# Block-sparse attention and a gated MLP on one core: how the first head pair is loaded and masked, and how the in-projection is dealt out

## The chip, the core and the metric

The kernel runs on one core of a Trainium2 chip. The core has a matrix engine (TensorE, PE in the profile; its weight loads are PEld), a vector engine (DVE), a scalar engine for activations (ACT), a general engine (POOL) and an engine that here only issues transfers (SP). Each engine works through its own list of instructions in order and waits on semaphores for the others. Transfers are issued from the list of SP or of ACT and are carried out by 16 DMA engines. [...]

The metric is the device time of one execution in microseconds (us). The kernel before took 222.43 us, the median of 13 runs (221.78 to 223.98).

## The reference

Attention over 4 batches, 8 heads, 768 positions and 64 dimensions, with a mask in blocks of 32, and then a gated MLP whose spatial matrix mixes the positions:

```python
scores = scale * np.matmul(q, k.transpose(0, 1, 3, 2))
mask = np.abs(blk_i - blk_j) <= 1
mask = mask | (blk_i == 0) | (blk_j == 0) | (blk_i == n_blocks - 1) | (blk_j == n_blocks - 1)
for qb in range(n_blocks):
    for kb in sampled_blocks[qb]:            # 3 for each of 24 blocks
        mask[qb*block:(qb+1)*block, kb*block:(kb+1)*block] = True
attn = softmax(np.where(mask, scores, -1e9))
x = np.matmul(attn, v)                       # heads side by side: (4, 768, 512)

h = np.maximum(x @ w_in, 0.0)                # 512 -> 1024
u, v = h[..., :512], h[..., 512:]
v_n = (v - mean(v)) / np.sqrt(var(v) + 1e-6)
v_s = np.einsum('ts,bsd->btd', w_spatial, v_n) + b_spatial[None, :, None]
out = (u * v_s) @ w_out
```

## The kernel before, in words

**Attention.** q and k of a head pair are loaded as fp32 with positions on partitions (st_q, st_k, 128x768 for two heads), cast to bf16 (nat_q, nat_k) and transposed to 64 dimensions by 768 positions (qt, kt). The first batch is transposed on PE (tr_head for pair 0, one head at a time; tr_pair in three thirds for pairs 1 to 3), later pairs by DMA (tr_dma and split_pair). The mask is part of the matmul: below the 64 dimensions, qt and kt have 24 more rows. In kt they hold ind, which says which key block a position is in; in qt they hold bm times ind, where the 24x24 matrix bm is 0 for an allowed pair of blocks and -300 for any other. All heads need the same rows. Before the change ind is built on POOL (memset, affine_select) and rearranged by DVE; bm is worked out by DVE from iotas and the sampled blocks (allowed, samp_f); two matmuls make qt's rows in PSUM (mq), ACT copies them into head 0, and mask_rows (DVE, heads 1 to 5 in part) and mask_dma (SP queue, heads 4 to 7 of kt and 6 and 7 of qt) repeat them for the other heads.

**Order of the attention.** The first batch (N0 = 48 steps g) works by halves of the queries: qk_exp_half(g) makes two score matmuls 88x128 by 88x384 and one exponential of 128x768 on ACT; steps 0 to 2 belong to head 0, 3 to 5 to head 1, and so on to step 23; steps 24 to 47 repeat this for the second half of the queries. av_half runs 6 steps behind (LAG0), and xtr_half transposes the normalised result of a pair (xn) to xt. Later batches use qk_exp with whole heads, six steps for each head, and av 7 steps behind (LAG).

**The MLP.** moe_units(b) lists the matmuls of a batch's MLP as units, 108 for each batch: twelve in-projections of 4 units (v0 to v5 and u0 to u5, one for each 128 positions), six spatial products of 6, six out-projections of 4. The string order gives the sequence of the in-projections. They take turns at two PSUM banks (tags moe0 and moe1), which the transposes use too. v_post copies a v product to vsb with a ReLU and takes its mean and variance (DVE: vsb, stats, mv); after v2 and v5, POOL makes rstd for three of them, and normalize (DVE, vn) is queued in norm_q with the number of products that must be done before it. normalize_next is called in the middle of every product and after every u. u_post copies a u product to un, on ACT except for u0 of batch 0.

**How units are dealt out.** In the first batch one unit goes to each step from g = 29 on. At the change of batch none is dealt in steps 48 to 54; from g = 55 (N0 + 7) the 89 that are left are spread over 50 steps. Batches 1 and 2 spread 108 over 48 and 52 steps; the last batch's MLP runs after the attention, back to back, over six banks.

**The start.** The first tiles of pair 0 are loaded by heads: head 0 of k and q on ACT's queue, samp_i and head 1 on SP's. keep_warm issues matmuls on a tile of zeros, whose result nobody reads: 8 of 512 columns first, 6 of 128 after the q transposes, and 2 of 128 in each of the first six steps.

These lines set the order at the two places that the change touches:

```python
keep_warm(8, 512)                                       # L199
...
tr_head(0, "k", dve_copy)                               # L281
act_copy(kt[0][D:KR, :], ind)
...                                                     # mq, two matmuls, act_copy into qt[0]
tr_head(0, "q", dve_copy)
keep_warm(6, 128)
...
norm_q.extend((i, products[0] + 2) for i in range(tcc - 2, tcc + 1))   # L496
...
if g == N0 + 7:
    slots_left = 50                                     # L682
```

Of the kernel before, what the change touches and what calls it, by code (L numbers as in the profile page):

```python
# [10 lines left out]
FP32 = mybir.dt.float32  # L11
BF16 = mybir.dt.bfloat16
I32 = mybir.dt.int32
# [13 lines left out]
def kernel(  # L27
# [146 lines left out]
    nc.scalar.dma_start(out=stk[:, 0:1], in_=dram(k, 0, 0, 1))  # L174
    nc.scalar.dma_start(out=stq[:, 0:1], in_=dram(q, 0, 0, 1))
    nc.sync.dma_start(out=samp_i, in_=_listify(sampled_blocks).bitcast(I32))
    nc.sync.dma_start(out=stk[:, 1:2], in_=dram(k, 0, 1, 1))
    nc.sync.dma_start(out=stq[:, 1:2], in_=dram(q, 0, 1, 1))
# [6 lines left out]
    allowed = const.tile([NB, NB], FP32)  # L185
    tiny = const.tile([128, 1], FP32)
    nc.vector.memset(warm, 0.0)
    nc.gpsimd.memset(ind_nat, 0.0)
# [5 lines left out]
    def keep_warm(n, cols):  # L194
        for _ in range(n):
# [3 lines left out]
    keep_warm(8, 512)  # L199
# [4 lines left out]
    nc.gpsimd.affine_select(out=ind_nat, in_=ind_nat, compare_op=ALU.not_equal, fill=1.0,  # L204
                            base=0, pattern=[[-1, NB], [0, BLK]], channel_multiplier=1)
# [6 lines left out]
    colidx = const.tile([NB, NB], FP32)  # L212
    nc.gpsimd.iota(colidx, pattern=[[1, NB]], base=0, channel_multiplier=0,
                   allow_small_or_imprecise_dtypes=True)
    make_identity(nc, ident)
    for s in range(NG):
        nc.gpsimd.memset(vv[s][:, :, :, D:VA], 1.0)
    nc.gpsimd.memset(mhalf, -0.5)

    nat_tile(0, "q"), nat_tile(0, "k")  # L220
    nc.vector.tensor_copy(out=ind, in_=ind_nat.rearrange("b (p c) -> b c p", c=NCH))
# [3 lines left out]
    nc.vector.tensor_scalar(out=edge, in0=edge, scalar1=0.0, scalar2=None, op0=ALU.is_equal)  # L225
    nc.vector.tensor_tensor(out=diff, in0=diff, in1=diff, op=ALU.mult)
    nc.vector.tensor_scalar(out=allowed, in0=diff, scalar1=1.0, scalar2=edge,
                            op0=ALU.is_le, op1=ALU.max)
    nc.vector.memset(allowed[:, 0:1], 1.0)
    nc.vector.memset(allowed[:, NB - 1:NB], 1.0)  # L230
    samp_f = const.tile([NB, 2 * NR], FP32)
    nc.vector.tensor_copy(out=samp_f, in_=samp_i)
    for r in range(NR):
        nc.vector.scalar_tensor_tensor(out=allowed, in0=colidx,
                                       scalar=samp_f[:, 2 * r:2 * r + 1], in1=allowed,
                                       op0=ALU.is_equal, op1=ALU.max)
    bm = const.tile([NB, NB], BF16)
    nc.vector.tensor_scalar(out=bm, in0=allowed, scalar1=1.0, scalar2=-MASK_NEG,
                            op0=ALU.subtract, op1=ALU.mult)
    cast_qk(0, "q", slice(0, 1), nc.vector)  # L240
    cast_qk(0, "k", slice(0, 1), nc.scalar)
# [39 lines left out]
    tr_head(0, "k", dve_copy)  # L281
    act_copy(kt[0][D:KR, :], ind)
    mq = psum.tile([128, 1024], FP32, tag="sc", bufs=2, name="mq")
    for hf in range(2):
        nc.tensor.matmul(out=mq[0:NB, hf * 512:hf * 512 + HALF], lhsT=bm,
                         rhs=ind[:, hf * HALF:(hf + 1) * HALF], start=True, stop=True)
    act_copy(qt[0][D:KR, :].rearrange("p (b c) -> p b c", b=2),
             mq[0:NB].rearrange("p (b c) -> p b c", b=2)[:, :, 0:HALF])
# [150 lines left out]
    def moe_units(b):  # L439
# [19 lines left out]
        def normalize_next():  # L459
            if norm_q and norm_q[0][1] <= products[0]:  # L460
                normalize(norm_q.popleft()[0])

        def add(n, operands, post):
# [4 lines left out]
            def step(i):  # L468
# [5 lines left out]
                if i == n // 2:  # L474
                    normalize_next()
# [5 lines left out]
        def v_post(tcc, ps):  # L481
# [8 lines left out]
            if tcc % 3 == 2:  # L490
# [5 lines left out]
                norm_q.extend((i, products[0] + 2) for i in range(tcc - 2, tcc + 1))  # L496
# [7 lines left out]
        def u_post(tcc, ps):  # L504
            if b == 0 and tcc == 0:
# [4 lines left out]
            normalize_next()  # L510

        def in_proj(tcc, cols, post):
# [5 lines left out]
                 "v0 v1 u0 v2 u1 v3 u2 v4 v5 u3 u4 u5")  # L518
# [53 lines left out]
    def mask_rows(nm, h0, h1):  # L572
        t = kt_all if nm == "k" else qt_all
        nc.vector.tensor_copy(out=t[D:KR, h0:h1, :],
# [160 lines left out]
```

## Time and profile before

| | |
|---|---|
| median of 13 runs | 222.43 us (221.78 to 223.98) |
| the profiled execution | 223.36 us, span 221.6 us |
| PE busy | 213.0 us of the span |
| ACT busy | 177.0 us |
| DVE busy | 135.9 us |
| POOL busy | 66.9 us |
| first exponential begins | 8.72 us |
| first score matmul of step 48 begins | 45.60 us |

The span runs from the first to the last instruction; the time of the execution also holds what lies around it. A view with a start and a duration is a timeline: start, duration, engine, line, operation, output and inputs, count, and in brackets how long the engine was idle before it and which instruction released it. The profile models the ends of matmuls, so successive matmuls overlap in the figures. Line numbers of helpers stand for all their callers: L472 is every MLP matmul, L313 and L348 are score matmuls of later batches and of the first, L262 a head's transposes, L196 a warmer, L124 a cast, L574 and L579 are the copies and transfers of mask rows.

### The profile page before, as it was taken

How to read it: one execution, taken by the hardware profiler on the slowest of the kernel's cores; microseconds unless marked ns; L12 is line 12 of the kernel's file. 1: busy time of each engine (PE TensorE's matmuls, PEld its weight loads, DVE VectorE, ACT ScalarE, POOL GpSimd, SP SyncE). 2: the span in 40 equal slices, each digit the busy share in tenths (PEclk: the TensorE clock that was granted, in tenths of full speed). 3: DMA queues.
4: the chain of work that ended last, by engine and by line, in shares of the span. 5: the costliest groups of instructions: out<-in, count | busy, mean ns of one | idle time of the engine just before them, and what ended most of it. 6: DMA issues, size and time to landing. Idle time of an engine off the chain costs nothing.

```text
span 221.6 us, 5292 instructions
## 1 busy us (share of the span) xinstructions
PE 213.0 (96%) x2122; PEld 127.7 (58%) x2122; DVE 135.9 (61%) x302; ACT 177.0 (80%) x245; POOL 66.9 (30%) x89
## 2 busy tenths in 40 slices
PE   7989999999999999999899999999899999999993
PEld 2567666665666666666465656565565565544551
DVE  5488527856886635377798635376896433675532
ACT  5489999999999889988979878888989885266351
POOL 6457879523187040400609001200602000022000
PEclk9999999999999999999999999999999999999999
DMA  6999999999995498979772369998321124620016
GB/s 179 336 300 394 397 264 340 171 117 315 237 366 113 113 275 181 276 249 268 219 186 108 72 131 230 219 280 211 62 48 26 37 50 84 221 91 0 0 54 230
DMA packets 59460, 41.26 MB, mean 186 GB/s; under 512 B 42524, under 2 KB 54956, under 8 KB 59436
## 3 DMA queue, kind: packets, MB, share of 16 engines
q1 hardware_dynamic: 59148, 40.54, 69.8%
q10 hardware_dynamic: 288, 0.39, 0.6%
q8 instruction: 16, 0.26, 0.5%
q14 instruction: 8, 0.07, 0.1%
HBM read 24.38 MB, written 6.29 MB: 138 GB/s over the span
## 4 chain that ended last, share of the span: by engine, by line
PE 84%; DVE 8%; ACT 5%; issue 1%; POOL 1%; ACTq 0%; POOLq 0%
PE ps_moe L472 32%; PE ps L313 18%; PE ps_av L329 11%; PE ps L348 7%; ACT a_all L317 4%; PE ps_t L472 4%; PE ps_sc L472 4%; PE ps_av L364 3%; PE wps L196 2%; DVE kt_all L278 2%; DVE kt_all L302 1%; PE ps_moe L262 1%; DVE vsb L485 1%; DVE vn L499 1%; DVE qt_all L278 1%
## 5 line engine op out<-in xcount | busy, mean ns | idle before, releaser
L317 ACT ACTIVATE a_all<-ps 128x768 bf16<-128x768 f32 x144 | 114.6, 815 | 16.1 <-PE ps L313 7.4
L313 PE MATMUL ps<-qt_all,kt_all 88*128 88x384 bf16 x288 | 70.3, 325 | 0.8 <-ACT a_all L317 0.7
L329 PEld LDWEIGHTS <-a_all 128*128 128x128 bf16 x864 | 46.1, 97 | 35.6 <-issue 2.2
L329 PE MATMUL ps_av<-vv,a_all 128*128 128x65 bf16 x864 | 50.8, 194 | 0.0
L472 PE MATMUL ps_moe<-w_in_t,xt 128*128 128x512 bf16 x160 | 48.8, 379 | 1.4 <-DVE vsb L485 1.3
L352 ACT ACTIVATE a_all<-ps 128x768 bf16<-128x768 f32 x48 | 35.5, 813 | 3.5 <-PE ps L348 3.2
L472 PE MATMUL ps_moe<-vn,w_spt 128*128 128x512 bf16 x120 | 35.4, 378 | 0.0
L472 PEld LDWEIGHTS <-xt 128*128 128x128 bf16 x192 | 18.6, 97 | 16.3 <-DVE xt L386 0.5
L492 POOL TENSOR_SCALAR std<-mv 128x3 f32<-128x3 f32 x8 | 1.9, 241 | 82.3 <-DVE mv L489 73.3
L535 DVE SCALAR_TENSOR_TENSOR gn<-ps_moe,b_col,un 128x512 bf16<-128x512 f32 x20 | 15.0, 749 | 17.1 <-PE ps_moe L472 16.9
L348 PE MATMUL ps<-qt_all,kt_all 88*128 88x384 bf16 x96 | 23.8, 330 | 1.2 <-DVE qt_all L278 0.7
L124 POOL CAST nat_k<-st_k 128x768 bf16<-128x768 f32 (+1 forms) x14 | 11.5, 819 | 41.2 <-DMA st_k<-in_k_dram 32.4
L472 PE MATMUL ps_moe<-w_out_t,gt 128*128 128x512 bf16 x80 | 23.1, 378 | 0.1
L313 PEld LDWEIGHTS <-kt_all 88*128 88x128 bf16 x288 | 19.3, 98 | 1.6 <-issue 1.0
L472 PEld LDWEIGHTS <-w_spt 128*128 128x128 bf16 x144 | 13.7, 97 | 10.6
L364 PEld LDWEIGHTS <-a_all 128*128 128x128 bf16 x288 | 15.1, 98 | 6.2
L488 DVE BATCH_NORM_STATS2 stats<-vsb 128x6 f32<-128x512 bf16 x24 | 16.6, 693 | 1.5 <-ACT vsb L483 0.8
L364 PE MATMUL ps_av<-vv,a_all 128*128 128x65 bf16 x288 | 17.0, 194 | 0.0
L499 DVE TENSOR_SCALAR vn<-vsb,mv,rstd 128x512 bf16<-128x512 bf16 x24 | 12.8, 560 | 5.0 <-POOL rstd L494 4.8
L485 DVE TENSOR_SCALAR vsb<-ps_moe 128x512 bf16<-128x512 f32 x18 | 12.3, 686 | 5.3 <-PE ps_moe L472 4.7
L555 DVE COPY osb<-ps_moe 128x512 f32<-128x512 f32 x10 | 6.9, 692 | 11.5 <-PE ps_moe L472 11.4
L395 DVE TENSOR_TENSOR xn<-ps_av,rc 128x384 bf16<-128x384 f32 x24 | 13.4, 557 | 0.8
(98 smaller groups left out, 219.7 us busy)
## 6 DMA issues: line engine op xcount, KB each, us to landing
out_dram<-osb SPq DMA_DIRECT2D x24, 256.0 KB, 2.7
st_v<-in_v_dram SPq DMA_DIRECT2D x14, 384.0 KB, 5.8
st_k<-in_k_dram SPq DMA_DIRECT2D x13, 384.0 KB, 4.7
st_q<-in_q_dram SPq DMA_DIRECT2D x13, 384.0 KB, 3.9
wst<-in_moe_w_spatial_dram SPq DMA_DIRECT2D x3, 768.0 KB, 9.6
wst<-in_moe_w_in_dram SPq DMA_DIRECT2D x4, 512.0 KB, 8.6
wst<-in_moe_w_out_dram SPq DMA_DIRECT2D x2, 512.0 KB, 7.5
wst<-in_k_dram SPq DMA_DIRECT2D x2, 384.0 KB, 9.2
```

The costliest lines, as they stand in the source:

```text
L313: nc.tensor.matmul(out=ps[:, hf * 512:hf * 512 + HALF], lhsT=kt[j % H][:, ci * 128:(ci + 1) * 128], rhs=qt[j % H][:, hf * HALF:(hf + 1) * ...
L317: nc.scalar.activation(out=a_ref[j][:, ci, :].rearrange("p (b c) -> p b c", b=2), in_=ps.rearrange("p (b c) -> p b c", b=2)[:, :, 0:HALF], ...
L329: nc.tensor.matmul(out=av_ref[j][:, qc, :], lhsT=a_ref[j][:, ci, qc * 128:(qc + 1) * 128], rhs=vv[p % NG][:, h, ci, :], start=(ci == 0), s ...
L348: nc.tensor.matmul(out=ps[:, u * 512:u * 512 + HALF], lhsT=kt[j][:, ci * 128:(ci + 1) * 128], rhs=qt[j][:, grp * HALF:(grp + 1) * HALF], s ...
L352: nc.scalar.activation(out=a_ref["half", gh][:, 2 * i:2 * i + 2, :], in_=ps.rearrange("p (b c) -> p b c", b=2)[:, :, 0:HALF], func=AF.Exp, ...
L364: nc.tensor.matmul(out=av_ref["half", gh][:, qc, :], lhsT=a_ref["half", gh][:, ci, qc * 128:(qc + 1) * 128], rhs=vv[p][:, h, ci, :], start ...
L395: nc.vector.tensor_tensor(out=xn_ref[p][:, :, h, :], in0=ps[:, :, 0:D], in1=rc.to_broadcast([128, NCH, D]), op=ALU.mult)
L472: nc.tensor.matmul(out=box[0], lhsT=lhs, rhs=rhs, start=(i == 0), stop=(i == n - 1))
L485: nc.vector.tensor_scalar(out=vsb[:, tcc, :], in0=ps, scalar1=0.0, scalar2=None, op0=ALU.max)
L488: nc.vector.bn_stats(out=stats, in_=vsb[:, tcc, :])
L499: nc.vector.tensor_scalar(out=vn[:, tcc, :], in0=vsb[:, tcc, :], scalar1=mv[:, tcc, 0:1], scalar2=rstd[:, tcc:tcc + 1], op0=ALU.subtract, ...
L535: nc.vector.scalar_tensor_tensor(out=gn[:, tcc, :], in0=ps, scalar=b_col[:, tcc:tcc + 1], in1=un[:, tcc, :], op0=ALU.add, op1=ALU.mult)
```

## The change

- Pair 0 is loaded whole: k on ACT's queue, q on SP's behind samp_i.
- ind_nat's memset moves from POOL to DVE; POOL's iotas come before its affine_select; ACT rearranges ind in place of DVE.
- bm is made from a static part that does not depend on the samples, and one comparison of all three samples, a maximum and one more operation.
- The two mask products are issued apart, the first before head 0's transposes; k of head 0 is cast on DVE and its transposed form copied by ACT.
- kt's mask rows of heads 1 to 3 are copied by POOL, those of 4 to 7 by one transfer straight from ind. qt's rows are copied by DVE by halves of the queries, at the start and in steps 6, 20 and 23.
- Warmers: 6 of 512 for 8, 3 of 128 added after the first mask product, none in steps 0 to 2. Both of head 1's transposes come in step 0, pair 1's in steps 1 and 2.
- In-projection units are dealt in steps 48 to 55 too, none in step 56, and the 81 left over 48 steps from step 57.
- norm_q counts half products: the first three normalisations become due one product later, the last three half a product earlier. u1 and u2 of batch 0 go to DVE. Batches 1 and 2 alternate v and u to the end.

```diff
-    nc.scalar.dma_start(out=stk[:, 0:1], in_=dram(k, 0, 0, 1))
-    nc.scalar.dma_start(out=stq[:, 0:1], in_=dram(q, 0, 0, 1))
+    nc.scalar.dma_start(out=stk, in_=dram(k, 0, 0, 2))
     nc.sync.dma_start(out=samp_i, in_=_listify(sampled_blocks).bitcast(I32))
-    nc.sync.dma_start(out=stk[:, 1:2], in_=dram(k, 0, 1, 1))
-    nc.sync.dma_start(out=stq[:, 1:2], in_=dram(q, 0, 1, 1))
+    nc.sync.dma_start(out=stq, in_=dram(q, 0, 0, 2))
...
-    nc.gpsimd.memset(ind_nat, 0.0)
+    nc.vector.memset(ind_nat, 0.0)
...
-    keep_warm(8, 512)
+    keep_warm(6, 512)
...
-    nat_tile(0, "q"), nat_tile(0, "k")
-    nc.vector.tensor_copy(out=ind, in_=ind_nat.rearrange("b (p c) -> b c p", c=NCH))
...
-    nc.vector.tensor_scalar(out=allowed, in0=diff, scalar1=1.0, scalar2=edge,
+    nc.vector.tensor_scalar(out=static, in0=diff, scalar1=1.0, scalar2=edge,
                             op0=ALU.is_le, op1=ALU.max)
-    samp_f = const.tile([NB, 2 * NR], FP32)
-    nc.vector.tensor_copy(out=samp_f, in_=samp_i)
-    for r in range(NR):
-        nc.vector.scalar_tensor_tensor(out=allowed, in0=colidx,
-                                       scalar=samp_f[:, 2 * r:2 * r + 1], in1=allowed,
-                                       op0=ALU.is_equal, op1=ALU.max)
+    nc.vector.tensor_scalar(out=static, in0=static, scalar1=1.0, scalar2=-MASK_NEG,
+                            op0=ALU.subtract, op1=ALU.mult)
+    for c in (0, NB - 1):
+        nc.vector.memset(static[:, c:c + 1], 0.0)
+    nat_tile(0, "q"), nat_tile(0, "k")
+    nc.scalar.activation(out=ind, in_=ind_nat.rearrange("b (p c) -> b c p", c=NCH),
+                         func=AF.Copy)
+    hit = const.tile([NB, NR, NB], FP32)
+    nc.vector.tensor_tensor(
+        out=hit, in0=colidx.to_broadcast([NB, NR, NB]),
+        in1=samp_i.rearrange("b (r t) -> b r t", t=2)[:, :, 0:1].to_broadcast([NB, NR, NB]),
+        op=ALU.is_equal)
+    hits = const.tile([NB, NB], FP32)
+    nc.vector.tensor_reduce(out=hits, in_=hit.rearrange("b r n -> b n r"), op=ALU.max,
+                            axis=mybir.AxisListType.X)
     bm = const.tile([NB, NB], BF16)
-    nc.vector.tensor_scalar(out=bm, in0=allowed, scalar1=1.0, scalar2=-MASK_NEG,
-                            op0=ALU.subtract, op1=ALU.mult)
-    cast_qk(0, "q", slice(0, 1), nc.vector)
-    cast_qk(0, "k", slice(0, 1), nc.scalar)
+    nc.vector.scalar_tensor_tensor(out=bm, in0=hits, scalar=0.0, in1=static,
+                                   op0=ALU.is_equal, op1=ALU.mult)
+    nc.scalar.activation(out=kt[0][D:KR, :], in_=ind, func=AF.Copy)
+    cast_qk(0, "k", slice(0, 1), nc.vector)
+
+    def kt_mask(h):
+        nc.gpsimd.tensor_copy(out=kt[h][D:KR, :], in_=ind)
+
+    def qt_mask(h0, h1, grp):
+        cols = slice(grp * HALF, (grp + 1) * HALF)
+        nc.vector.tensor_copy(out=qt_all[D:KR, h0:h1, cols],
+                              in_=qt_all[D:KR, 0:1, cols].to_broadcast([NB, h1 - h0, HALF]))
...
+    cast_qk(0, "k", slice(1, 2), nc.gpsimd)
...
-    tr_head(0, "k", dve_copy)
-    act_copy(kt[0][D:KR, :], ind)
     mq = psum.tile([128, 1024], FP32, tag="sc", bufs=2, name="mq")
-    for hf in range(2):
+
+    def mask_product(hf):
         nc.tensor.matmul(out=mq[0:NB, hf * 512:hf * 512 + HALF], lhsT=bm,
                          rhs=ind[:, hf * HALF:(hf + 1) * HALF], start=True, stop=True)
-    act_copy(qt[0][D:KR, :].rearrange("p (b c) -> p b c", b=2),
-             mq[0:NB].rearrange("p (b c) -> p b c", b=2)[:, :, 0:HALF])
+        act_copy(qt[0][D:KR, hf * HALF:(hf + 1) * HALF],
+                 mq[0:NB, hf * 512:hf * 512 + HALF])
+
+    mask_product(0)
+    keep_warm(3, 128)
+    cast_qk(0, "q", slice(0, 1), nc.vector)
+    tr_head(0, "k", act_copy)
+    mask_product(1)
     tr_head(0, "q", dve_copy)
     keep_warm(6, 128)
...
-        def normalize_next():
-            if norm_q and norm_q[0][1] <= products[0]:
+        def normalize_next(time):
+            if norm_q and norm_q[0][1] <= time:
                 normalize(norm_q.popleft()[0])
...
-                    normalize_next()
+                    normalize_next(2 * products[0])
...
-                norm_q.extend((i, products[0] + 2) for i in range(tcc - 2, tcc + 1))
+                norm_q.extend((i, 2 * products[0] + (6 if tcc == 2 else 3)) for i in range(tcc - 2, tcc + 1))
...
-            if b == 0 and tcc == 0:
+            if b == 0 and tcc < NCH // 2:
...
-            normalize_next()
+            normalize_next(2 * products[0] + 1)
...
-                 "v0 v1 u0 v2 u1 v3 u2 v4 v5 u3 u4 u5")
+                 "v0 v1 u0 v2 u1 v3 u2 v4 u3 v5 u4 u5")
...
-    cast_qk(0, "k", slice(1, 2), nc.gpsimd)
+    kt_mask(1)
     cast_qk(0, "q", slice(1, 2), nc.gpsimd)
+    kt_mask(2)
     prepare(1, "kq")
     cast_v(0)
-    mask_rows("k", 1, 2)
-    mask_rows("q", 1, 2)
-    mask_dma("k", 4, H)
+    kt_mask(3)
+    qt_mask(1, 4, 0)
+    nc.sync.dma_start(out=kt_all[D:KR, 4:H, :],
+                      in_=ind.rearrange("b (o n) -> b o n", o=1).to_broadcast([NB, H - 4, S]))
     load(1, "v")
     load(3, "kq")
-    mask_dma("q", 6, H)
...
-    for p, slots in ((1, (2, 2, 2, 3, 4, 4)), (2, (7, 7, 8, 9, 9, 10)),
+    for p, slots in ((1, (1, 1, 1, 2, 2, 2)), (2, (7, 7, 8, 9, 9, 10)),
...
-        if g < 6:
+        if 3 <= g < 6:
             keep_warm(2, 128)
-        if g < 2:
-            tr_head(1, "kq"[g], dve_copy)
+        if g == 0:
+            tr_head(1, "k", dve_copy)
+            tr_head(1, "q", dve_copy)
...
-        if g == 1:
-            mask_rows("k", 2, 4)
-            mask_rows("q", 2, 4)
-        if g == 5:
-            mask_rows("q", 4, 6)
+        if g in (6, 20, 23):
+            qt_mask(*{6: (4, 8, 0), 20: (1, 4, 1), 23: (4, 8, 1)}[g])
...
-            if g == N0 + 7:
-                slots_left = 50
+            if g < N0 + 9 and g != N0 + 8:
+                moe_q.popleft()()
+            if g == N0 + 9:
+                slots_left = 48
```

## The prediction

> **What bounds the kernel now.** I read the page's totals and slices first, then the chain of work that ended last, then busy time by stretches, then the timeline at the stretches where TensorE (PE) is not full.
>
> ```profile
> span 221.6 us, 5292 instructions
> PE 213.0 (96%) x2122; PEld 127.7 (58%) x2122; DVE 135.9 (61%) x302; ACT 177.0 (80%) x245; POOL 66.9 (30%) x89
> ...
> PE 84%; DVE 8%; ACT 5%; issue 1%; POOL 1%; ACTq 0%; POOLq 0%
> ```
>
> PE is the bound, and the chain is on it for 84%. So a gain must come from PE time that is empty, drawn out, or waiting. Busy time by stretches shows where (columns: stretch, its length, then busy time and instructions of PE, PEld, DVE, ACT, POOL, clock, DMA share, GB/s):
>
> ```profile
> 5.00:10.00 5.00, 4.99 (x32) 2.86 (x30) 2.66 (x8) 1.61 (x2) 2.10 (x4) 1.00 1.00 336
> ...
> 45.50:51.00 5.50, 4.73 (x61) 3.22 (x58) 2.68 (x11) 5.15 (x8) 0.79 (x1) 1.00 0.99 139
> ...
> 103.00:112.00 9.00, 8.31 (x90) 4.93 (x87) 6.52 (x14) 7.85 (x12) 3.69 (x5) 1.00 0.83 215
> 153.00:162.00 9.00, 8.37 (x90) 4.99 (x89) 6.79 (x13) 7.87 (x12) 3.70 (x5) 1.00 0.40 79
> ```
>
> The reader is to see four places. From 5 to 10 us PE is busy with only 32 instructions, long ones, ahead of the first exponential. From 45.5 to 51 us ACT is full (5.15 of 5.5) and PE has room. Around 110 and 160 us PE lacks some 0.65 us each. The timeline names their causes:
>
> ```profile
> 1.17 3.60 PE L196 MATMUL wps<-warm 128*128 128x512 bf16 x8 [1.17 <-DVE tiny L189]
> 4.70 0.85 PE L262 MATMUL ps_moe<-ident,nat_k 128*64 128x128 bf16 x6
> 5.56 0.81 PE L285 MATMUL mq<-ind,bm 24*24 24x384 bf16 x2
> 6.30 0.85 PE L262 MATMUL ps_moe<-ident,nat_q 128*64 128x128 bf16 x6
> ...
> 8.72 0.81 ACT L352 ACTIVATE a_all<-ps 128x768 bf16<-128x768 f32 x1 [1.51 <-PE ps L348]
> 10.25 0.81 ACT L352 ACTIVATE a_all<-ps 128x768 bf16<-128x768 f32 x1 [0.72 <-PE ps L348]
> ...
> 14.76 19.73 ACT L352 ACTIVATE a_all<-ps 128x768 bf16<-128x768 f32 x27 [0.52 <-PE ps L348]
> ```
>
> ```profile
> 107.18 0.90 DVE L499 TENSOR_SCALAR vn<-vsb,mv,rstd 128x512 bf16<-128x512 bf16 x1 [1.32 <-POOL rstd L494]
> ...
> 109.86 0.67 DVE L485 TENSOR_SCALAR vsb<-ps_moe 128x512 bf16<-128x512 f32 x1
> ...
> 110.58 0.38 PE L472 MATMUL ps_moe<-w_in_t,xt 128*128 128x512 bf16 x1 [0.69 <-DVE vsb L485]
> ...
> 160.59 0.38 PE L472 MATMUL ps_moe<-w_in_t,xt 128*128 128x512 bf16 x1 [0.63 <-DVE vsb L485]
> ```
>
> In the last view VectorE (DVE) sits before vn until POOL has rstd; the copy vsb that frees PE's bank is queued behind vn, and PE waits for it.
>
> **The change part by part: the start.** Until 8.72 PE is an unbroken row: 8 warmers to 4.77, k transposes, two mask products, q transposes, 6 warmers, the first scores at 7.88. Afterwards two warmers are gone (2 x 0.45 = 0.9, PE free near 3.9), one mask product goes ahead of the transposes, and the k transposes wait for a whole first tile instead of its half. When that lands (T) no row says. The 192 KB half landed after 2.5 us (3.2 us on the clock); a whole st_k has a median of 4.7 us, which gives 0.72 + 4.7 = 5.4. The earliest is 3.8, the half plus another 192 KB at the 350 GB/s of later stretches. I take 4.6, the middle, near the rows at 4.75 to 4.85 where three halves had landed. Far end: the 9.2 us of a staged load, T = 9.9.
>
> From T: DVE cast 0.34 and hand-over 0.06, k transposes 0.78, second mask product 0.40, q transposes 0.78, warmers 0.75 (DVE's copy of 0.55 beside them), scores 0.84 to the exponential: T + 3.95 = 8.55 against 8.72. The q tile must land by T + 1.2 = 5.8; it is issued at 1.23, and at 4.7 us it is there at 5.9, 0.1 late at most. The mask: DVE's static part is ready when iotas are (five small operations of 0.15 to 0.25); hit, maximum and bm are three of at most 0.3 in place of a cast, three of 0.29 to 0.31 and one of 0.17 (5.34 at present), so bm is out by 4 if samp_i, first on the SP queue, lands by 3. ACT takes over ind (0.84 in place of DVE's 0.66), done near 3.6; its mask copy ends near 4.5, and its k copy (0.8) and two half mask copies (0.5 each) run beside PE's transposes.
>
> Between exponentials 0 and 6 the old trace loses 1.8 us (8.72 + 6 x 0.705 = 12.95 against 14.76; 0.705 is ACT's pitch from 25 to 31 us). The last piece is DVE: two mask-row copies of 0.55, then copies of pair 1 until qt at 14.18. The change takes kt's rows from DVE to POOL and halves qt's, so qt of head 2 is ready near 12.7. But both head-1 transposes (0.78 each, still long) now stand ahead of scores 1: 8.49 + 1.56 gives scores near 10.05, exponential 1 at 10.6 (0.35 later than before), 2 at 11.35, 3 at 12.1 behind the two transpose groups of pair 1 (0.39 each), then 0.72 each: number 6 at 14.3. Gain 0.5; I take **0.4**. Bounds: T = 3.8 gives +1.3, T = 5.4 gives -0.3.
>
> PE's speed: the same six transposes take 0.85 at 8.83 and 0.52 at 10.26. PE has been at it since 1.17, so the shorter durations came 8.5 to 9 us after the first matmul, though the granted clock reads 1.00 throughout. With gaps of some 0.3 us before T it may come later: six more slow groups at twice 0.32 cost up to 1.2, so the start's lower end is **-0.8**.
>
> [...]
>
> **What moves queues.** Three kt_mask copies go to POOL: bounded by its 0.50 (128x384 cast) and 0.83 (128x768). They fit its waits for loads (1.06, 1.63, 0.98 us before casts), so they cost nothing; without that cover, 0.8 each ahead of q's second half or pair 1. ind_nat's memset leaves POOL (0.73) for DVE, idle there for 1.42. SP loses qt's mask transfer, issued at 9.53 for 0.82, so five loads are issued about 1 us sooner; the DMA engines are full (share 1.00 to 1.06 from 5 to 30 us), so I count no gain. The new qt_mask copies (0.41 to 0.55) fall at 13.5, 24.5 and 27 us, where DVE idles 1 us or more per head in the later two; in the first one they replace the 0.55 at 14.79.
>
> **The batch change.** Steps 48 to 54 now run without in-projection: PE needs 0.52, ACT sets 0.705. Step 55 and 56 then carry two units each (0.95, and 1.34 with the transposes and a wait for ACT's un). With one unit per step, PE needs 0.737, so it adds 0.03 x 5 = 0.14 until step 55 (51.02 for 50.88). Steps 55 and 56 take 0.74 and 0.70, so step 57 begins at 52.46 instead of 53.17: 0.71. And 27 units are done instead of 23, 4 x 0.215 = 0.86 less later, where PE is full. Together 1.57. Unit 27, the first to need the last transposed tile, may wait for the xt copy: at 33.15 the same arrangement cost 0.3; here the second step's scores lie between, so 0.1 to 0.3. DVE takes two un copies (0.69 each) from ACT (0.60) in a stretch where it idles 1.3 per head; it then has some 10 us of work from 50.5 to 62 us, so up to 0.5 of bank waits could come. I take **1.4**, ends 0.9 and 1.6.
>
> **The order of the middle batches.** The stalls cost more than their idle figures: PE's next matmul stood ready at 109.74 and 159.81 and began at 110.58 and 160.59, 0.84 + 0.78 = 1.62. With vn0 a product later, DVE does at 105.9 what lies before vsb: at 110 xn (ready 107.5, to 108.25), kt's two copies (1.24, to 109.4), vsb to 110.05, still 0.35 late, gain 0.5. At 160 the 0.8 of vn goes and vsb ends at 159.8, gain 0.7. Sum **1.2**; ends 0.3 (xn and copies slow beside POOL casts, such as 1.80 for a pair of copies) and 1.6. The later group's vn now comes after 4 units, about 1.8 us, where rstd needs 2.9 (0.69, 0.69, 0.18, 0.23, 0.9 and hand-overs): DVE waits 1.1. Behind it stand xn and later gn, whose banks no v product needs by then; un is on ACT. It costs nothing, and 0.5 if a norm falls there. In the last batch PE has no gap from 193 to 217, and only vn0 to vn2 move: 0.
>
> Sum: 0.4 + 1.4 + 1.2 = 3.0, less 0.1 for the unpriced waits: **2.9**. The profiled execution took 223.36 us (span 221.6), 0.93 above the median 222.43 of 13; what makes it longer than the median is not shown, so I take the difference off the median: **219.5** (220.5 for an execution like the profiled one).
>
> **Rivals.**
> - The start loses: T late or the shorter durations later, -0.8 in place of +0.4. For it: no row has a whole tile in competition, and exponential 1 has more ahead of it. Against: pair 1's loads land no later. Time 220.7.
> - DVE's wait is only moved: the busier vector queue at 50 to 62 us and around 110 and 160 us gives 1.2 back. For it: copies of 1.2 to 1.9 us beside POOL. Against: vn is the one instruction there that waits for POOL. 220.7.
> - Slower: the whole first tile lands as late as a staged load, T = 9.9. The first exponential then comes at 9.9 + 3.95 = 13.85, 5.1 late; the other two parts keep 2.5: 222.43 + 5.1 - 2.5 = 225.0. It decides from T = 7.3, where 2.5 is used up. For it: q tiles of 384 KB took 9.4. Against: those stood behind seven others in the queue, this is first in its own.
> - No effect: the loads, not PE, set the early pace, and later waits for them take all back: 222.4. Against: ACT idles 0 from 14.76 to 34.5.
>
> **How the numbers follow.** Forecast 0.56 (own range 218.4 to 220.6, from the ends of its terms, not all at once), start 0.18, wait moved 0.14, slower 0.08, no effect 0.04. A tenth of the two middle cases crosses 221.8. A measurement tells 0.3% (0.67 us) from no change. So faster 0.85, same 0.06, slower 0.09. The range goes from 218.2 to 222.2.
>
> **What would show it.** Right: exponential 0 at 8.2 to 9.0 and number 6 before 14.5; one ps_moe matmul per step at 46 to 51 us; no PE wait for vsb over 0.4 near 108 and 157. Wrong: st_k landing after 5.5, six-transpose groups of 0.85 after 11 us, PE waiting for un or vsb at 50 to 60 us.

## The result, and the profile after

The changed kernel took 220.61 us, the median of 11 executions (218.53 to 221.11), beside 222.59 us for the kernel before, the median of 48 (221.70 to 224.66). The ratio is 0.9878, with a 95% interval of 0.9850 to 0.9906: faster by 1.2%. That is near the ratio of the means (220.22 and 222.94); the medians alone make 0.9911, faster by 0.9%. The ratios here and below leave out executions that lie over 1.5% above the fastest of their kernel. The profiled execution took 220.91 us (span 219.1), where that of before took 223.36 (221.6), so the two traces account for 2.45 us, 2.5 of it in the span.

The page of the kernel after: span, busy time by engine, and the share of each engine in the chain of work that ended last.

```profile
span 219.1 us, 5276 instructions
PE 211.9 (97%) x2117; PEld 127.3 (58%) x2117; DVE 135.7 (62%) x302; ACT 176.9 (81%) x245; POOL 68.7 (31%) x91
...
PE 82%; DVE 12%; ACT 2%; DMA 1%; issue 1%; SPq 1%; POOL 1%; DVEq 0%; POOLq 0%
```

PE is the bound as before. DVE's part of the chain has risen from 8% to 12%, and most of its new pieces lie between 52 and 66 us: a wait of PE for DVE stands at their end. Busy time by stretches of the kernel after (stretch, length, then busy time and instructions of PE, PEld, DVE, ACT, POOL, clock, DMA share, GB/s):

```profile
5.00:10.00 5.00, 5.00 (x35) 3.32 (x35) 2.63 (x5) 2.17 (x4) 3.51 (x5) 1.00 1.01 331
45.50:51.00 5.50, 5.50 (x68) 3.62 (x67) 3.76 (x12) 5.41 (x8) 0.05 (x1) 1.00 1.06 206
60.00:70.00 10.00, 9.47 (x100) 5.74 (x99) 7.69 (x12) 8.96 (x14) 7.69 (x9) 1.00 0.82 212
...
103.00:112.00 9.00, 8.43 (x84) 4.92 (x83) 7.11 (x17) 7.49 (x11) 3.57 (x5) 1.00 0.72 183
...
153.00:162.00 9.00, 9.00 (x93) 5.41 (x92) 8.03 (x19) 8.21 (x13) 3.70 (x5) 1.00 0.35 67
```

From 45.5 to 51 us PE is now full, 68 instructions for 61. The hole near 157 us is closed, the one near 109 us is not, and there is a new one between 60 and 70 us, where PE was busy for 9.95 us before. The timeline of the kernel after at the start:

```profile
3.92 0.36 DVE L124 CAST nat_k<-st_k 128x384 bf16<-128x384 f32 x1
4.40 0.50 PE L193 MATMUL wps<-warm 128*128 128x128 bf16 x3
4.83 0.85 PE L274 MATMUL ps_moe<-ident,nat_k 128*64 128x128 bf16 x6
4.90 0.85 DVE L124 CAST nat_q<-st_q 128x384 bf16<-128x384 f32 x1 [0.61 <-DMA st_q<-in_q_dram]
...
8.35 0.81 ACT L369 ACTIVATE a_all<-ps 128x768 bf16<-128x768 f32 x1 [1.33 <-PE ps L365]
...
10.51 5.03 ACT L369 ACTIVATE a_all<-ps 128x768 bf16<-128x768 f32 x7 [1.35 <-PE ps L365]
```

The first exponential comes 0.37 earlier, the second 0.26 later, and from there seven follow at 0.70 apart, so that number 6 falls near 14.0 instead of 14.76. And the timeline where the new wait is, with POOL beside it:

```profile
59.45 0.89 POOL L511 TENSOR_TENSOR rstd<-std,mhalf 128x3 f32<-128x3 f32 x1
60.30 0.82 POOL L124 CAST nat_k<-st_k 128x768 bf16<-128x768 f32 x1
60.37 2.56 DVE L516 TENSOR_SCALAR vn<-vsb,mv,rstd 128x512 bf16<-128x512 bf16 x3 [1.33 <-POOL rstd L511]
...
63.54 1.24 DVE L319 COPY kt_all<-tt_k 64x768 bf16<-64x768 bf16 x2
64.52 0.95 POOL L127 CAST vv<-st_v 128x768 bf16<-128x768 f32 x1
64.81 1.98 DVE L319 COPY qt_all<-tt_q 64x768 bf16<-64x768 bf16 x2
65.73 0.50 PE L330 MATMUL ps<-qt_all,kt_all 88*128 88x384 bf16 x2 [0.53 <-DVE qt_all L319]
```

DVE stands 1.33 us in front of the first vn until POOL has rstd, then does all three vn, and the copies of the next pair's kt and qt come behind them. PE reaches the first scores of that pair before qt is there. The trace of before at the same place:

```profile
62.94 1.24 DVE L302 COPY kt_all<-tt_k 64x768 bf16<-64x768 bf16 x2
64.20 1.65 DVE L499 TENSOR_SCALAR vn<-vsb,mv,rstd 128x512 bf16<-128x512 bf16 x2
65.77 1.86 DVE L302 COPY qt_all<-tt_q 64x768 bf16<-64x768 bf16 x2
```

There kt went ahead of vn, and the first of the two copies of qt ended near 66.7 (half of 1.86 after 65.77), some 0.1 us before the scores that needed it began at 66.80. There was hardly any room for qt to come later.

The lead of the changed kernel over the old one, read from the same instruction in both traces, tells where each part was won: 0.74 at step 48 (45.60 against 44.86), 1.57 at step 57 (53.17 and 51.60), and there PE has four units more behind it, 0.86. At the copy of the last transposed tile of the second batch (97.32 and 95.61) the lead is 1.7, not the 2.4 that 1.57 and 0.86 make: the new wait took 0.7. (PE is idle for 0.53 there, but the scores begin 0.88 after the product ahead of them, at 64.85, where 0.19 is usual: 0.69 late.) At the last in-projection (202.47 and 199.85) it is 2.6.

### The profile page after: what moved, and what is told of

Its sections match the earlier page's. It is cut to its first block, busy times and chain, and to the rows that moved or that the text cites. A ratio compares the mean times of both kernels' runs of the same rounds, so it can differ in the third digit from the quotient of the medians.

```text
span 219.1 us, 5276 instructions
## 1 busy us (share of the span) xinstructions
PE 211.9 (97%) x2117; PEld 127.3 (58%) x2117; DVE 135.7 (62%) x302; ACT 176.9 (81%) x245; POOL 68.7 (31%) x91
## 4 chain that ended last, share of the span: by engine, by line
PE 82%; DVE 12%; ACT 2%; DMA 1%; issue 1%; SPq 1%; POOL 1%; DVEq 0%; POOLq 0%
PE ps_moe L489 31%; PE ps L330 18%; PE ps_av L346 10%; PE ps L365 7%; PE ps_t L489 4%; PE ps_sc L489 4%; PE ps_av L381 4%; DVE vn L516 1%; PE ps_moe L274 1%; ACT a_all L369 1%; DMA xt<-xn 1%; DVE kt_all L319 1%; DVE vsb L502 1%; DVE kt_all L290 1%; DVE stats L505 1%
## 5 line engine op out<-in xcount | busy, mean ns | idle before, releaser
L489 PE MATMUL ps_moe<-w_in_t,xt 128*128 128x512 bf16 x160 | 49.3, 379 | 0.7 <-DVE vsb L502 0.6
L489 PEld LDWEIGHTS <-w_spt 128*128 128x128 bf16 x144 | 13.7, 97 | 10.6
L516 DVE TENSOR_SCALAR vn<-vsb,mv,rstd 128x512 bf16<-128x512 bf16 x24 | 11.8, 528 | 4.8 <-POOL rstd L511 4.8
L411 DVE RECIPROCAL rc<-ps_av 128x6 f32<-128x6 f32 x24 | 4.5, 186 | 15.6 <-PE ps_av L346 15.6
```

The costliest lines, as they stand in the source:

```text
L489: nc.tensor.matmul(out=box[0], lhsT=lhs, rhs=rhs, start=(i == 0), stop=(i == n - 1))
L516: nc.vector.tensor_scalar(out=vn[:, tcc, :], in0=vsb[:, tcc, :], scalar1=mv[:, tcc, 0:1], scalar2=rstd[:, tcc:tcc + 1], op0=ALU.subtract, ...
```

## The experiments

Two theories were put to the test. A: the start, the earlier units at the batch change and the order add up, each at the size that the traces show, and the wait near 66 us costs 0.7. B: they do not add; a stall that is taken away comes back at the next late thing. For the kernels below I give, besides the ratio, two instants of the one profiled execution of each: *a*, the start of the first product of probabilities with v (it holds what the start is worth), and *z*, the start of the last group of in-projections. z - a holds what lies between, without the start.

| kernel | a | z | z - a | ratio to before (95%) |
|---|---|---|---|---|
| before | 14.56 | 202.47 | 187.91 | 1 |
| start_only | 13.80 | 201.65 | 187.85 | 0.9969 (0.9941 to 0.9998) |
| mlp_only | 13.27 | 200.41 | 187.14 | 0.9917 (0.9884 to 0.9951) |
| after | 13.80 | 199.85 | 186.05 | 0.9878 (0.9850 to 0.9906) |
| after_again | 13.88 | 199.82 | 185.94 | 0.9873 (0.9831 to 0.9914) |
| deal_undone | 12.13 | 202.04 | 189.91 | 0.9985 (0.9930 to 1.0040) |
| order_undone | 12.09 | 198.34 | 186.25 | 0.9872 (0.9828 to 0.9916) |
| order_again | 12.71 | 199.06 | 186.35 | 0.9896 (0.9862 to 0.9930) |
| norm_undone | 13.53 | 201.59 | 188.06 | 0.9998 (0.9966 to 1.0031) |
| string_undone | 13.64 | 199.77 | 186.13 | 0.9886 (0.9845 to 0.9928) |
| early_split | 13.49 | 199.75 | 186.26 | 0.9952 (0.9911 to 0.9993) |
| early_split2 | 13.82 | 198.45 | 184.63 | 0.9834 (0.9795 to 0.9873) |
| best | 12.56 | 199.96 | 187.40 | 0.9949 (0.9913 to 0.9985) |
| warm16 | 14.27 | 203.08 | 188.81 | 0.9975 (0.9941 to 1.0009) |

### The start alone, and the MLP's part alone

start_only is the changed kernel with these lines put back; mlp_only is the kernel before with the lines of the changed kernel taken over at the same places, and with norm_q counting in half products. The parts between two "..." are called hunks below.

```diff
-            if g < N0 + 9 and g != N0 + 8:
-                moe_q.popleft()()
-            if g == N0 + 9:
-                slots_left = 48
+            if g == N0 + 7:
+                slots_left = 50
...
-            if b == 0 and tcc < NCH // 2:
+            if b == 0 and tcc == 0:
...
-            normalize_next(2 * products[0] + 1)
+            normalize_next(2 * products[0])
...
-                norm_q.extend((i, 2 * products[0] + (6 if tcc == 2 else 3)) for i in range(tcc - 2, tcc + 1))
+                norm_q.extend((i, 2 * products[0] + 4) for i in range(tcc - 2, tcc + 1))
...
-                 "v0 v1 u0 v2 u1 v3 u2 v4 u3 v5 u4 u5")
+                 "v0 v1 u0 v2 u1 v3 u2 v4 v5 u3 u4 u5")
```

> The start of the changed kernel with the MLP of the kernel before: units dealt from step 55 over 50 steps, norm_q and the order of the middle batches as before, only u0 of batch 0 on DVE. Theory A (the parts add): the lag of 0.74 us that the two traces show at step 48 reaches the end, so the span is 220.9 and the median some 0.7 below before's. Theory B (the start only changes how soon PE's matmuls become short, and that varies from run to run): the median is within 0.3 of before's, and the single times spread over more than 2 us.

> The start of the kernel before with the changed MLP dealing, normalisation times, order, and u1 and u2 of batch 0 on DVE. Theory A (the parts add): 1.8 us less than before (2.5 of span less 0.7 of the start), with PE waiting some 0.5 us for qt_all near 66 us as in the changed kernel. Theory B (the later DVE waits come only when the steps before them are early): the wait near 66 us is gone, and the gain is 2.4.

start_only's profiled execution has a span of 220.9 us, 0.7 less than before; by the ratio it is 0.7 us as well (0.0031 of 222.4). All of it is there at a (0.76), and z - a is that of before. The median tells less: 222.28 us (220.83 to 223.35), beside 222.44 for before in the same series, so 0.2, with times that spread over 2.5 us. That is what theory B expected, and the interval of the ratio all but touches 1: the times alone show the start's gain barely, if at all. mlp_only (median 221.28) has a span of 219.5, so 2.1 less, though 0.8 of it only is in z - a; its profile also shows short matmuls already from 4.60 us on, 5 us sooner than the profile of before, and its a is 1.29 earlier. Among the profiles that are short so early, the old start (mlp_only) has its a at 13.27, and the new one has it at 12.09 to 12.71 (order_undone, deal_undone, best, order_again): the new start is ahead there too, by 0.6 to 1.2. The waits of PE in mlp_only (place, releaser, then total, times and longest in us):

```profile
PE ps L313 <- DVE qt_all L302: 1.0, 1, 1.0
...
PE ps_moe L472 <- DVE vsb L485: 0.6, 1, 0.6
```

The wait for qt_all near 66 us is there without the new start, so it belongs to the MLP's part. The two ratios together give 0.9886, the changed kernel 0.9878: by the ratios they add, as A says, but intervals of about 0.003 either way (0.7 us) leave room for losses. The profiles do not add: z - a falls by 0.8 in mlp_only and by 1.9 in the changed kernel. The trace of mlp_only has the 1.1 that is missing. 0.2 is lost before step 48 (at 44.55, 31.28 after a, where the changed kernel takes 31.06); 0.3 at step 50 (its scores begin 1.02 after those of step 49, for 0.74); 0.3 near 58.5, where the second matmul of a pair of units comes late (the pair takes 0.88, for 0.59); and the wait near 66 us is 0.5 longer (1.00 for 0.53), of which 0.15 is won back on the way. What holds PE up at the first three places was not sought.

> The changed kernel itself, beside the three that are compared with it. Theory A (two things vary from run to run by 1 to 2 us each: when PE's matmuls become short, and whether a DMA transpose of gn is late): the times again fall into groups some 1.5 to 2 us apart, and the median is 220 to 221. Theory B (one chip differs from another): all times in one group.

It gave 220.24 us (219.56 to 220.88), span 219.1 again, with the same two waits (0.3 near 66 us, 0.6 near 109). The median is what A expected; its groups 1.5 us apart were not seen in these six.

### The units at the batch change, and the order

deal_undone puts back the first hunk above alone; order_undone puts back the last three together (the normalisations' due times and the order of u and v); order_again is order_undone a second time.

> The changed kernel with the dealing at the batch change undone: no units in steps 48 to 54, and the 89 left over 50 steps from step 55. Theory A (the dealing is worth 1.57 of PE time and gives 0.7 back to the wait for qt_all near 66 us): the wait is gone or under 0.2, and the span is 219.1 + 0.9 = 220.0. Theory B (the wait comes from the new due time of the normalisations alone): the wait stays, and the span is 219.1 + 1.6 = 220.7.

> The changed kernel with the due times of the normalisations and the order of the middle batches as before. Theory A (the order is worth 0.1 at the second batch and 0.8 at the third, and the due time of v3 to v5 costs 0.7 at the first): PE waits 0.6 to 0.7 for vsb at the second and third batch, the wait for qt_all near 66 us shrinks, and the span is 219.1 + 0.9 - 0.7 to 219.1 + 0.9, 219.3 to 220.0. Theory B (the due time has no part in the wait near 66 us, DVE is full there): wait unchanged, span 220.0.

> The kernel without the edit of order once more, unchanged, to see whether its 217.6 us came from an early start of the short matmuls (they were short from 4 us on in its profile, from 10 us in the changed kernel's). Theory A (the wait near 66 us is gone without the new due times, whenever the matmuls become short): if they become short near 10 us, span 219.0 to 219.3 with no wait for qt_all; if near 4 us, 217.6 again. Theory B (the wait was missing only because TensorE ran 1.3 us ahead): with short matmuls from 10 us the wait for qt_all is there, 0.5 or more, and the span 219.8.

From start_only (neither) to order_undone and order_again (units dealt, old order) z - a falls from 187.85 to 186.25 and 186.35: the earlier units, with u1 and u2 of batch 0 on DVE, are worth 1.55 us. From there to the changed kernel (186.05 and 185.94) it falls by 0.3 more: that is all that the whole edit of order is worth in the traces. The medians show no gain at all: 220.07 and 220.55 us without the edit, 220.24 and 220.61 with it; a difference of 0.3 is below what they can tell. The low span of order_undone, 217.6, is its early a: 217.6 + (13.80 - 12.09) = 219.3. order_again's, with short matmuls from about 5.3 us, is 218.3, and + 1.09 that makes 219.4.

In both kernels with the old order the wait near 66 us is absent, though PE comes to that place earlier there than in the changed kernel (a of 12.09 and 12.71). order_again did not become short near 10 us, as its test asked; norm_undone below comes close to it (old due times, the same units, a of 13.53), and the wait is absent there too. So it is not a matter of PE's lead: theory A. The old waits for vsb are both back (order_again, PE's waits after 100 us, two stretches):

```profile
PE ps_moe L489 <- DVE vsb L502: 0.7, 1, 0.7
...
PE ps_moe L489 <- DVE vsb L502: 0.6, 1, 0.6
```

So the edit of order takes away the idle 0.6 near 157 us and some 0.1 near 109, and brings its own wait near 66 us in exchange.

deal_undone was worse than either theory had it. Its new due times meet a first batch that is behind with its units: PE comes to the scores near 64 us and waits 1.65, and then its clock drops to 0.52. Busy time of deal_undone by stretches of 2 us (the third number from the end is the granted clock):

```profile
64.00:66.00 2.00, 0.35 (x4) 0.22 (x4) 1.97 (x3) 0.74 (x2) 2.00 (x3) 1.00 1.16 316
66.00:68.00 2.00, 2.00 (x12) 1.02 (x11) 1.33 (x3) 0.83 (x2) 1.61 (x2) 0.52 0.57 126
68.00:70.00 2.00, 2.00 (x14) 1.01 (x13) 0.18 (x2) 1.06 (x2) 0.00 (x0) 0.63 0.03 8
70.00:72.00 2.00, 2.00 (x27) 1.31 (x26) 0.70 (x1) 1.86 (x3) 0.00 (x0) 1.00 0.03 6
```

For some 3.5 us PE did half its instructions, some 1.7 us lost. Of the 3.9 by which z - a exceeds the changed kernel's (186.05), this and the longer wait (1.65 against 0.53) make 2.8; 1.1 is left for the units that are dealt later. The one execution whose mean clock was 1.000 took 221.28 us, the profiled one (0.989) 223.08; but one at 0.997 took 223.01, so the clock is not the whole of the difference.

### Due times or sequence?

norm_undone puts back the due times alone (the third and fourth hunk above), string_undone the sequence of u and v alone (the last hunk).

> The changed kernel with the old due times of the normalizations in every batch (the first group after 4 half-products, the later one after 4, where the changed kernel has 6 and 3), and with the new order of u and v. Theory A (the wait near 66 us comes from the later group's due time: half a product earlier puts the three vn of 0.85 us on VectorE ahead of the copies of the next pair's kt and qt): no wait of TensorE for qt_all between 60 and 70 us, the wait for vsb near 109 us stays at 0.6 to 0.7, the one near 157 stays away. Span 218.4 where the matmuls become short near 10 us as in the changed kernel, 217.0 where they do so near 4 us; median 219.7. Theory B (it comes from the earlier in-projection alone, whatever the due times): the wait for qt_all stays, 0.5 to 1.6; span 219.1 or more, median 220.4 to 220.9.

> The changed kernel with the old order of u and v in the middle batches alone (v4 v5 u3 u4 u5 at the end in place of v4 u3 v5 u4 u5); the due times are new. Theory A: the wait for qt_all near 66 us stays at 0.3 to 1.0, since its batch has another order that nothing touched; the waits for vsb are two again, 0.7 near 109 us and 0.6 near 157 us. Span 219.8 where the matmuls become short near 10 us, 218.4 where near 4 us; median 220.9. Theory B (the order of u and v is worth nothing, the due times took the third batch's wait away): no wait near 157 us, span 219.1, median 220.4.

string_undone is the changed kernel over again: z - a 186.13, waits of 0.60 near 66 us and 0.57 near 109, none near 157. So it is the due times that closed the hole near 157 us, as B had it for this run; beside the new due times the sequence gave 0.1 to 0.2.

norm_undone has no wait near 66 us, as A expected, but at 220.9 us it is 2.5 above the span that A gave, and its median of 222.86 is no better than before's. Both waits for vsb are there: 0.69 near 108 us and, against A, 0.64 near 160, so the new sequence without the new due times closes no hole. Beside the old due times it costs 1.8 (z - a of 188.06 against 186.25 and 186.35). The timeline of norm_undone at the two batch changes:

```profile
59.50 1.73 DVE L516 TENSOR_SCALAR vn<-vsb,mv,rstd 128x512 bf16<-128x512 bf16 x2 [1.33 <-POOL rstd L511]
...
61.84 0.73 DVE L319 COPY kt_all<-tt_k 64x768 bf16<-64x768 bf16 x2
62.59 0.82 DVE L516 TENSOR_SCALAR vn<-vsb,mv,rstd 128x512 bf16<-128x512 bf16 x1
63.33 1.87 DVE L319 COPY qt_all<-tt_q 64x768 bf16<-64x768 bf16 x2
...
118.61 1.24 DVE L319 COPY kt_all<-tt_k 64x768 bf16<-64x768 bf16 x2
119.86 0.82 DVE L516 TENSOR_SCALAR vn<-vsb,mv,rstd 128x512 bf16<-128x512 bf16 x1
120.73 0.38 PE L489 MATMUL ps_moe<-vn,w_spt 128*128 128x512 bf16 x1 [1.54 <-DVE vn L516]
```

With the old due times the last vn is queued behind xn and kt's copies. Near 63 us that lets kt and qt through in time. Near 120 us, where the new sequence makes v5 one product later, the spatial product needs that vn and stands still for 1.54. The same queue serves two customers, the scores (kt and qt) and the spatial product (vn), and each due time puts one behind the other.

### Taking the wait near 66 us away

The scores' customers can be served sooner instead. early_split issues the copies of pair 6 four and five steps earlier (k and q), and those of kt for every later pair two steps earlier; early_split2 does it for pairs 6 and 10 alone, those at the two holes.

```diff
-            if p + 1 < NP and s in (7, 9):
-                split_pair(p + 1, "k" if s == 7 else "q")
+            ks, qs = (7, 9) if p == 4 else (3, 4) if p == 5 else (5, 9)
+            if p + 1 < NP and s in (ks, qs):
+                split_pair(p + 1, "k" if s == ks else "q")
```

In early_split2 the first added line is this one:

```diff
+            ks, qs = (7, 9) if p == 4 else (3, 4) if p == 5 else (5, 9) if p == 9 else (7, 9)
```

> The changed kernel with the copies of the DMA-transposed k and q of the next pair (split_pair) issued earlier: in the fifth pair's steps 3 and 4 in place of 7 and 9, and k in step 5 in place of 7 for the later pairs. Theory A (the PE waits of 0.53 near 65.7 and 0.57 near 108.8 come from split_pair standing behind vn and rstd in DVE's queue): both waits go and the time falls by 1.2 to 1.5 against the changed kernel. Theory B (DVE is simply full there, and the waits only move): PE waits as long for another DVE result, and the time is within 0.3 of the changed kernel's.

> The changed kernel with split_pair earlier at two places only: steps 3 and 4 of the fifth pair, and k in step 5 of the tenth; the eleventh pair's k stays in step 7, because in the version that moved it too PE waited 1.3 us for vn behind it. Theory A: no wait of PE for DVE is left between 50 and 185 us, the span is 217.7 (219.1 less 0.7 and 0.7), and the median 1.0 to 1.4 below the changed kernel's. Theory B (the waits only move): a wait of 0.5 or more appears at another place, and the median is within 0.3.

early_split has no wait at 60 to 70 or 100 to 110 us, but waits for vn twice near 119 us, 1.3 in all and 0.9 the longer, where the changed kernel has none (its waits of PE):

```profile
PE ps_moe L489 <- DVE vn L516: 1.3, 2, 0.9
```

There theory B held: k of pair 11, moved forward, is copied at 116.20 for 1.87 us, behind the first vn and in front of the other two. The median was 222.19 us (220.60 to 225.06), no better than the changed kernel's. early_split2 has no wait of PE for another engine from 13 us to the end. Its timeline near 60 us, and its busy time at the three places:

```profile
59.01 0.69 DVE L319 COPY kt_all<-tt_k 64x768 bf16<-64x768 bf16 x2
59.71 0.72 DVE L319 COPY qt_all<-tt_q 64x768 bf16<-64x768 bf16 x2
60.51 2.53 DVE L516 TENSOR_SCALAR vn<-vsb,mv,rstd 128x512 bf16<-128x512 bf16 x3
```

```profile
60.00:70.00 10.00, 10.00 (x109) 6.17 (x108) 5.62 (x11) 9.63 (x14) 7.23 (x9) 1.00 0.89 211
100.00:110.00 10.00, 10.00 (x104) 5.98 (x102) 7.40 (x19) 9.21 (x14) 3.50 (x5) 1.00 0.87 226
...
153.00:162.00 9.00, 9.00 (x99) 5.57 (x98) 7.70 (x17) 8.54 (x13) 3.49 (x5) 1.00 0.35 67
```

The copies of kt and qt now fill the time in which DVE waited for rstd, and they take 0.69 and 0.72 instead of 1.24 and 1.98: POOL's casts there begin at 60.41, when they are all but done. The span is 217.7, what theory A gave, 1.4 less than the changed kernel: 0.7 for each of the two waits. The time is 219.27 us (219.05 to 219.52), ratio 0.9834, below both kernels; all six executions lie under all six of after_again, the changed kernel beside it. Three of the eleven of the first series of the changed kernel lie lower (218.53 to 219.11), and the intervals of the ratios overlap, so the surer sign is the traces: from the same a (13.82 for 13.80 and 13.88), z - a is 1.3 to 1.4 shorter. It has the lowest median of these kernels.

best adds the old due times to early_split2.

```diff
-                norm_q.extend((i, 2 * products[0] + (6 if tcc == 2 else 3)) for i in range(tcc - 2, tcc + 1))
+                norm_q.extend((i, 2 * products[0] + 4) for i in range(tcc - 2, tcc + 1))
...
-            normalize_next(2 * products[0] + 1)
+            normalize_next(2 * products[0])
```

> The early split of two pairs that gave 219.27 us, with the old due times of the normalizations. Theory A: with the early split the copies of kt and qt for the second batch stand ahead of the three vn already, so the old due times add nothing: no wait of TensorE over 0.3 us from 13 us on, span 217.7 (216.3 where the matmuls become short near 4 us), median 219.2. Theory B (later vn now make the spatial product wait, as in the kernel that splits every pair early): a wait for vn of 0.5 to 0.9 near 66 or 110 us, span 218.3 to 218.6, median 219.9.

It took 221.71 us: the wait for vn near 119 us is back (1.5), as in norm_undone, and the one for vsb near 157 (0.6). B was right on its kind, and its size was twice that expected. The name fits early_split2, not this one.

### More warmers

```diff
-    keep_warm(6, 512)
+    keep_warm(16, 512)
```

> The changed kernel with 16 warmers of 512 columns in place of 6. Theory A (what makes the times spread is when PE's matmuls become short, and a longer unbroken row of warmers settles it): matmuls are short before the first transposes, the first exponential comes at 8 to 9 us, the single times lie within 1 us of each other, and the median is at or below the changed kernel's. Theory B (the row of warmers only delays PE): first exponential 2 us or more later than 8.35, median 1 to 2 us above the changed kernel's, spread unchanged.

All sixteen were issued as one row from 1.17 to 6.90, and the transposes behind them were short at once (six in 0.52 at 7.36). Yet exponential 0 came at 9.76, 1.4 later than in the changed kernel, because PE was still at its warmers when the first tile was cast; a is 14.27. What the row gained in short matmuls it lost in delay, and the median, 222.42 us, is 1.8 above the changed kernel's, as B expected. The profiled execution, 224.12 us, also holds a wait of its own:

```profile
PE ps_moe L489 <- DMA gt<-gn: 1.8, 1, 1.8
```

That late transposing transfer explains 1.8 of z - a there, and no other profile shows PE waiting so for it. Its cause was not sought. The spread of the times (220.91 to 226.45) was no smaller than that of the changed kernel, against A's expectation that the start's pace makes the spread.

## Why the prediction was right, and where it was wrong

The sign, the range (218.2 to 222.2) and the bound were right: 220.61 against 219.5. The sum was 2.9 and the traces show 2.5, in part by luck: the start and the batch change came out 0.5 above their terms together and the order 0.9 below its own, so the sum is nearer than its parts. The rest of the difference is the profiled execution of after, only 0.3 above its median, where I had taken the 0.93 by which that of before exceeded its median off both (220.5 was the forecast for such an execution, and it took 220.91).

- **Start: 0.4 predicted, 0.74 to 0.76 measured** in the traces (0.2 by the medians of start_only and before). The mechanism was right and the size off, with T mis-sized. T was 4.6 in the sum; DVE cast the tile at 3.92 without waiting for it. Of these 0.7 by which the tile was earlier, 0.2 arrived at exponential 0 (8.35 for 8.55), since the three warmers behind the first mask product hold the k transposes until 4.83, though the cast ended at 4.28. Exponential 1 came at 10.51, predicted 10.6, and number 6 near 14.0 for 14.3. The last six transposes of 0.85 began at 8.88, and from 10.27 on six take 0.53, where before they took 0.52 at 10.26: the short matmuls came no later, so in these executions the rival that the start loses is out, and so is the slower one (T = 9.9).
- **Batch change: 1.4 predicted, 1.55 measured** by order_undone and order_again against start_only. The 0.71 by step 57 and the 0.86 of the four units are in the trace (step 57 is 1.57 earlier with 0.74 from the start, which leaves 0.83; 27 units are done for 23).
- **Order: 1.2 predicted, 0.3 measured** in the traces and nothing in the medians. This is the step that failed. Near 157 us the 0.7 came, from the due times, as predicted. Near 109 us 0.5 was predicted and 0.1 came: kt's copies took 1.62 beside POOL's casts, where I had put 1.24. And the sentence that the wait for rstd at the later group "costs nothing, and 0.5 if a norm falls there" was wrong in the first batch. I had looked behind vn for xn and gn, and left out kt and qt of the next pair, which stand in the same queue; they cost 0.7 near 66 us. The trace of before had the row: there the copies of qt were already behind two vn, took 1.86 beside POOL's casts, and had some 0.1 us to spare.
- **The rival "DVE's wait is only moved"** was to give 1.2 back. It came true for the first batch's later group, at 0.7 of that 1.2, and with the 0.4 that did not come near 109 us it is why the order is worth so little.
- **Signs.** One unit per step from 46 to 51 us, exponential 0 inside 8.2 to 9.0, number 6 before 14.5: all seen. "No wait for vsb over 0.4 near 108 and 157" held at 157 (none) and failed near 108 (0.57).
- **When the matmuls become short.** The start's lower end, -0.8, rested on gaps ahead of T putting the shorter durations off; that was my estimate, and no run shows a gap doing it: in the profile of after PE waits for nothing from 1.17 us until they are short, and in order_again, where they were short before, a wait of 0.69 ahead of 6.52 left six transposes at 0.52. The profiles of the changed kernel had short matmuls from about 10.3 us on, and the runs with other edits from 4.0 to 10.3. That the profiles of before and after came within a microsecond of each other is luck, since four profiles with the changed start had them 5 to 6 us sooner.

What stays open: why the medians give the start 0.2 where the traces give it 0.7, and what holds PE up at the three places where mlp_only loses 0.2 to 0.3 us each.

## What to carry to other kernels

When a due time is moved, list every instruction behind the moved one in that engine's queue together with its customer on the bound engine, in each stretch where it occurs; a queue that is idle on average can still hold the next pair's operands behind a wait. Where two customers share a queue, serve the one that can go early while the queue waits anyway: here that took both waits away for 1.4 us, while moving the due times only traded one for the other. And look at durations beside the engine that runs at the same time, since the same copy took 0.7 or 2.0 us.

## What the runs showed of the hardware

**When matmuls become short varies between executions of one program.** With the granted clock at 1.00 from 0 to 13 us, six transposes take 0.85 us at first and 0.49 to 0.53 later (one group between). order_undone and order_again are one program; here are PE's timelines of the one, and of the other:

```profile
3.97 0.33 PE L296 MATMUL mq<-ind,bm 24*24 24x384 bf16 x1
4.23 0.34 PE L193 MATMUL wps<-warm 128*128 128x128 bf16 x3
4.50 0.52 PE L274 MATMUL ps_moe<-ident,nat_k 128*64 128x128 bf16 x6
```

```profile
4.39 0.50 PE L193 MATMUL wps<-warm 128*128 128x128 bf16 x3
4.82 0.75 PE L274 MATMUL ps_moe<-ident,nat_k 128*64 128x128 bf16 x6
5.50 0.33 PE L296 MATMUL mq<-ind,bm 24*24 24x384 bf16 x1
```

The first was short from about 4 us, the second from about 5.3, and the profiles of the changed kernel from about 10.3, all after the same row of warmers from 1.17. Of the eleven profiles with this row four became short between 4.0 and 5.3 us, seven between 9.6 and 10.4, and none between. In the four, a is 12.09 to 12.71, in the seven 13.49 to 13.88, so up to 1.8 us of an execution go with it. What sets the moment no profile shows.

**A wait of 1.65 us was followed by a clock of 0.52 and 0.63 for two stretches** of 2 us (deal_undone), while waits of 1.0 (mlp_only), 1.5 (best) and 1.54 (norm_undone) left it at 1.00 in the stretches of 2 us behind them, and in warm16, with a longer one of 1.8 between 100 and 150 us, its mean was 1.00 from 100 to 150 and from 150 to 217. So the length of the wait alone does not decide it; what does, one profile does not settle.

**DVE's bf16 copies and vn took about twice as long beside POOL's casts.** Two copies of kt took 0.69 to 0.73 without casts and 1.24 to 1.87 with them, two of qt 0.71 to 0.74 and 1.24 to 2.08, one vn 0.38 to 0.41 and 0.80 to 0.90. xn, which reads PE's product ps_av, took 0.56 in both cases. POOL's casts of 128x768 took 0.82 or 0.83 at the least and up to 1.04 beside the copies and vn, so they were slower there too; why, no row shows.
